# Mixing the first 128 queries by selection matmuls in a talking-heads attention kernel, and holding batch 0's score pairs to older gathers

## The chip, the cores and the metric

The kernel runs on one core of a Trainium2 chip. The metric is device time in microseconds (us) of one launch, the median over runs. TensorE is called PE, VectorE DVE, ScalarE ACT, GpSimd POOL and SyncE SP. DMA transfers are issued from the queues of SP, ACT and POOL and carried by the core's 16 DMA engines.

## The reference, cut to what matters

Attention in which the heads are mixed with each other twice (before and after the softmax), then a feed-forward layer with a squared ReLU:

```python
batch, n_heads, seq, head_dim = 8, 12, 448, 64
scores = (q @ k^T) / 8                                   # per head
scores = einsum('bhij,hg->bgij', scores, w_pre)          # heads mixed
attn = softmax(scores, axis=-1)
attn = einsum('bhij,hg->bgij', attn, w_post)             # heads mixed again
x = (attn @ v) as 3584 rows of 768
out = relu(x @ w_in)**2 @ w_out                          # 768 -> 2048 -> 768
```

## The kernel before, in words

**Score pairs.** `turn_unit` (L171) transposes q and k of two head pairs from the staged loads into PSUM (`tr_ps`); ACT copies qT and DVE copies kT to SBUF (L186). `score_pair` (L317) computes, for 128 queries and two heads, the scores of 448 keys: four matmuls (`s_ps`, L329), and two copies into the block `S` of 128 queries x 12 heads (L333, one on ACT, one on DVE). A block needs six pairs; three blocks of S are kept.

**Tiles and steps.** Mixing heads needs the heads of a query on the partition axis, whereas S has queries there. So the work goes by tiles of 10 queries (`IQ`), 45 tiles (`NT`) a batch. `gather` (L345) copies the 10 x 12 rows of a tile from S to a tile G by DMA, from SBUF to SBUF, 105 KB, on SP's queue (two of the first on ACT's). G has 8 buffers, and during the first 42 tiles (`HEAD`) six more, lent by the memory of a piece of w2 that is loaded later (`shared`, called w in the profile's rows).

A step handles two tiles. `mix` (L361) multiplies G by a block-diagonal form of w_pre (`pre`) into `m_ps` (four matmuls, L367), ACT takes the exp with its row sum (L372), DVE the reciprocal (L374), and POOL scales into `d` (L376). Two steps later (`LAG`) `unmix` (L388) multiplies by w_post and transposes (32 small matmuls, L399, `at_ps`); DVE copies into the attention tile (L404). When a part of a batch is complete, `av_unit` multiplies it by v (L199, `ot_ps`) and ACT copies to x^T (L210).

**Feed-forward.** `ffn1_unit` (L251, `h_ps`) and `ffn2_unit` (L281, `o_ps`) are cut into small units that fill TensorE in later steps, by a budget (`fill`). They use batch b's results while later batches are in attention. The weights w1 come in eight pieces, w2 in eight, over POOL's queue (`load_w1` L224, `load_w2` L236), each in a step that `at_load` names.

**Order.** PE and POOL run in the written order; DVE, ACT and SP take their instructions in program order. In each step: POOL's loads, timed units, `unmix` of two steps ago, score pairs or a turn, `mix`, gathers, `spin` (16 matmuls on the identity whose result nobody reads, in steps 0 to 9 and once before), then fillers. `scores_for` decides how many pairs a step computes, `gathers_for` issues gathers up to `gather_end`, 14 tiles ahead at first and 8 later. PSUM has eight banks, taken in turn under one tag, so a new tile waits for the reader of the tile eight allocations ago.

The lines that time the start's loads and gathers are few:

```python
HEAD = 3 * (AHEAD + 2 + MORE)                            # 42
eng = nc.scalar if k in (1, 3) else nc.sync              # gather's queue
at_load(-1 if x < 2 else 2, load_v, 0, x)                # pieces of V of batch 0
at_load(1 + x, load_w1, x)                               # w1, x = 2 to 7
if ds < PARTS[0][1] // 2 + LAG:
    spin(4)
```

Of the kernel before, what the change touches and what calls it, by code (L numbers as in the profile page):

```python
# [9 lines left out]
BF16 = mybir.dt.bfloat16  # L10
F32 = mybir.dt.float32
# [5 lines left out]
DMODEL = H * D  # L17
# [14 lines left out]
AHEAD = 6  # L32
LEAD = 14
MORE = 6
HEAD = 3 * (AHEAD + 2 + MORE)
OFF = 64 - H * (IQ // 2)
SCALE = 1.0 / 8.0
FIRST_TURN = (13, 14, 15)
# [6 lines left out]
def kernel(  # L45
# [46 lines left out]
    def wcol(w, name, eng, p0s):  # L92
# [4 lines left out]
            eng.dma_start(out=t[p0:p0 + HR, 0:H], in_=src)  # L97
        return t

    col_pre = wcol(w_pre, "col_pre", nc.sync, (OFF, 64))  # L100
    col_post = wcol(w_post, "col_post", nc.scalar, (0, 64))

# [25 lines left out]
    for t in dts:  # L128
        nc.vector.memset(t[:, S:DW], 0.0)

    shared = wts.tile([P, FT // 4 * DMODEL], BF16, name="w2_3", tag="w2_3", bufs=1)
    gts = [work.tile([P, S], BF16, name=f"G{x}") for x in range(AHEAD + 2)]
    more = [shared[:, S * x:S * x + S] for x in range(MORE)]
    for t in gts + more:
        nc.vector.memset(t[0:OFF, :], 0.0)

    def gather_tile(n):
        if n < HEAD:
            n = n % (AHEAD + 2 + MORE)
# [14 lines left out]
    w2 = [wts.tile([P, FT // 4, DMODEL], BF16, name=f"w2_{x}") for x in range(3)]  # L154

    qTs, kTs, bvecs, xts, h2ts, ats = {}, {}, {}, {}, {}, {}

# [30 lines left out]
    def av_unit(b, part, cp):  # L188
        at = ats[(b, part)]
        first = part == 0  # L190
        q0 = IQ * PARTS[b % 2][part]
        n = min(IQ * PARTS[b % 2][part + 1], S) - q0
# [43 lines left out]
    def load_w2(x):  # L236
        n = DFF // 8
        c = x % 2 * 2
        if x == 6:
            last = wts.tile([P, FT // 4 * DMODEL], BF16, name="w2_3", tag="w2_3", bufs=1)  # L240
            w2.append(last[:, :].rearrange("p (c m) -> p c m", m=DMODEL))
# [93 lines left out]
    def queries(t, y):  # L335
        return max(0, min(HQ, S - IQ * t - HQ * y))

    def span_of(s):
        b, t = s
        c = IQ * t  # L340
        return half_of(b, c) // 2, half_of(b, min(c + IQ, S) - 1) // 2

    def needs(s):
# [1 line left out]

    def gather(k):

        b, t = steps[k]
        c, end = IQ * t, min(IQ * t + IQ, S)
        g = gather_tile(k)  # L350
        eng = nc.scalar if k in (1, 3) else nc.sync
        row = OFF
        while c < end:
            n, z = divmod(half_of(b, c), 2)
            x = PR * z + c % PR
            m = min(end - c, P - x)
            eng.dma_start(out=g[row:row + H * m, :], in_=Sb[n][x:x + m, :, :])
            c, row = c + m, row + H * m
        Gs[k] = g

    def mix(k):  # L361
        pss = [bank("m_ps") for _ in range(2)]
        gs = [Gs.pop(2 * k + x) for x in range(2)]
        for y in range(2):
            for x in range(2):
                rows = slice(64 * y, 64 * y + H * queries(steps[2 * k + x][1], y) if y else 64)
                nc.tensor.matmul(pss[y][64 * x:64 * x + 64, 0:S], lhsT=pre[rows, :], rhs=gs[x][rows, :],  # L367
                                 start=True, stop=True)
        for y in range(2):
            e = work.tile([P, S], F32, name="e_sb", tag="E", bufs=3)  # L370
            sm = work.tile([P, 1], F32, name="sm", tag="sm", bufs=4)
            nc.scalar.activation(out=e[:, :], in_=pss[y][:, 0:S], func=ACT.Exp, scale=SCALE, accum_out=sm[:, 0:1])  # L372
            rc = work.tile([P, 1], F32, name="rc", tag="rc", bufs=4)
            nc.vector.reciprocal(out=rc[:, :], in_=sm[:, :])  # L374
            d = dts[(2 * k + y) % ND]
            nc.gpsimd.tensor_scalar(out=d[:, 0:S], in0=e[:, :], scalar1=rc[:, 0:1], scalar2=-1.0 / S,  # L376
                                    op0=ALU.mult, op1=ALU.add)
            dsb[(k, y)] = d

    def place_of(s):  # L380
        b, t = s
        part = sum(t >= x for x in PARTS[b % 2]) - 1
        if (b, part) not in ats:
            ats[(b, part)] = attn[(3 * b + part) % 2]
        return ats[(b, part)], 2 + IQ * (t - PARTS[b % 2][part])

    def unmix(k):

        places = [place_of(s) for s in steps[2 * k:2 * k + 2]]
        us = [bank("at_ps") for _ in range(2)]  # L390
        for y in range(2):
            d = dsb.pop((k, y))
            for r in range(VS):
                c = HR * (VS * y + r)
                for x in range(2):
                    rows = slice(64 * x, 64 * x + HR)
                    for z in range(2):
                        j = PR * (r + (R - VS) * z) if r or not z else S
                        nc.tensor.matmul(us[x][PR * z:PR * z + PR, c:c + HR], lhsT=d[rows, j:j + PR],  # L399
                                         rhs=post[rows, :], start=True, stop=True)  # L400
        for x, (at, c) in enumerate(places):
            src = us[x][:, 0:2 * VS * HR].rearrange("p (y m i) -> p m y i", y=2, i=HQ)
            dst = at[:, :, :, c:c + IQ].rearrange("p r g (y i) -> p (r g) y i", y=2)
            nc.vector.tensor_copy(out=dst, in_=src)  # L404

# [27 lines left out]
    with tc.manual_schedule(engines={PE, POOL}):  # L433
# [32 lines left out]
        issued, gathered = [NPAIR + 3], [0]  # L466
# [20 lines left out]
        def gathers_for(ds):  # L487
            while gathered[0] < min(gather_end(ds), len(steps)):
                if issued[0] < needs(steps[gathered[0]]):
                    break  # L490
                gather(gathered[0])
                gathered[0] += 1

        gathers_for(-1)
        for n in range(NPAIR, issued[0]):
            score_pair(n)
        spin(4)
        for f in loads.get(-1, []):
            f()
        for ds in range(nd + LAG):  # L500
            for i in (2 * ds, 2 * ds + 1):
                for f in loads.get(i, []):
# [19 lines left out]
            if old2:  # L522
                unmix(ds - LAG)
                for b1, t1 in old2:
                    ends = PARTS[b1 % 2]
                    if t1 + 1 in ends:
# [1 line left out]
                        for x, u in enumerate(av_units(b1, part)):  # L528
                            at_step(ds + (2 + x if b1 else 1), u)
                        if b1 == 0:  # L530
                            c = (IQ * ends[part], min(IQ * ends[part + 1], S))
# [57 lines left out]
```

The softmax here doesn't subtract the row's maximum and nothing guards it: scores larger than these inputs give would overflow.

## Time and profile before

| | |
|---|---|
| median of 13 runs | 588.24 us (583.74 to 594.48) |
| the profiled execution | 594.48 us, span 592.7 us |
| PE busy | 543.7 us (92%) |
| DVE, ACT, POOL busy | 407.4, 407.5, 399.0 us (69%, 69%, 67%) |
| DMA moved | 74.98 MB |
| chain that ended last | PE 77%, DMA 9%, ACT, DVE and POOL 3% each |
| q1 (SP's transfers) | 49.26 MB, 36.1% of 16 engines' span |
| q0 (POOL's loads) | 23.60 MB, 29.1% |
| G<-S from SP | 314 of 105.0 KB, and 15 into the lent memory |

The profile is one execution. "Busy" is the time in which an engine had an instruction at work; an idle gap is put down to what ended it (the releaser). The chain of waits goes back from the last instruction, at each step to what released it. A row of the timeline reads: start in us, length in us, engine, line of the kernel, operation, output and inputs, shape, count.

### The profile page before, as it was taken

The numbers are of one execution on the slowest core, as the hardware profiler recorded it, in microseconds if no ns is written. First come the engines' busy times: TensorE is split into PE (matmuls) and PEld (weight loads), VectorE is DVE, ScalarE is ACT, GpSimd is POOL, SyncE is SP. The second block draws the span as 40 slices with busy tenths as digits, with TensorE's granted clock in tenths as the row PEclk, the third lists the DMA queues.
The fourth block names the chain that finished last, engine by engine and source line by source line (L and its number), as shares of the span: only waits on it lengthen the run. The fifth ranks groups of instructions, "written<-read, shape, count | busy, mean of one in ns | idle before, by whom it ended". The sixth has DMA issues, their size and how long they took to land.

```text
span 592.7 us, 28172 instructions
## 1 busy us (share of the span) xinstructions
PE 543.7 (92%) x11810; PEld 310.7 (52%) x11810; DVE 407.4 (69%) x1050; ACT 407.5 (69%) x1223; POOL 399.0 (67%) x599
## 2 busy tenths in 40 slices
PE   3866698789799999999999999999999999999997
PEld 1543566554455556455555555545655555555554
DVE  5666488769777777776886777777777787765001
ACT  3656588678678866887678867896688768873420
POOL 5466559746658976788757955897678766892550
PEclk9889889889989999999999999999999999999999
DMA  9899868946974489547974599448953477442103
GB/s 138 135 219 184 179 123 146 182 82 120 202 155 93 85 163 183 115 85 123 175 157 85 98 181 184 94 86 156 182 129 78 82 145 159 82 83 56 41 11 83
DMA packets 83364, 74.98 MB, mean 127 GB/s; under 512 B 6436, under 2 KB 80164, under 8 KB 83236
## 3 DMA queue, kind: packets, MB, share of 16 engines
q1 hardware_dynamic: 51502, 49.26, 36.1%
q0 software_dynamic: 31264, 23.60, 29.1%
q8 instruction: 92, 1.51, 1.0%
q10 hardware_dynamic: 470, 0.32, 0.2%
q14 instruction: 36, 0.29, 0.1%
HBM read 47.20 MB, written 11.01 MB: 98 GB/s over the span
## 4 chain that ended last, share of the span: by engine, by line
PE 77%; DMA 9%; ACT 3%; DVE 3%; POOL 3%; issue 2%; ACTq 0%; DVEq 0%
PE o_ps L281 25%; PE h_ps L251 25%; PE at_ps L399 9%; PE ot_ps L199 6%; PE m_ps L367 6%; DMA G<-S 6%; PE s_ps L329 4%; PE tr_ps L182 2%; DMA w<-S 2%; DMA qkst<-in_q_dram 1%; POOL d L376 1%; DVE at L404 1%; ACT e_sb L372 1%; ACT xt L210 1%; POOL w L232 1%
## 5 line engine op out<-in xcount | busy, mean ns | idle before, releaser
L376 POOL TENSOR_SCALAR d<-e_sb,rc 128x448 bf16<-128x448 f32 x360 | 226.3, 639 | 154.2 <-DVE rc L374 153.0
L404 DVE CAST at<-at_ps 128x480 bf16<-128x480 f32 x360 | 219.8, 650 | 69.7 <-PE at_ps L399 63.3
L372 ACT ACTIVATE e_sb<-m_ps 128x448 f32<-128x448 f32 x360 | 195.6, 559 | 22.1 <-PE m_ps L367 16.7
L251 PE MATMUL h_ps<-xt,w 128*128 128x448 bf16 (+2 forms) x960 | 165.1, 321 | 1.9 <-DVE at L404 0.8
L281 PE MATMUL o_ps<-w,h 128*128 128x384 bf16 (+1 forms) x1024 | 163.2, 329 | 0.0
L260 POOL TENSOR_TENSOR h<-hr 128x448 bf16<-128x448 f32 (+2 forms) x136 | 113.7, 845 | 15.7 <-ACT hr L258 15.7
L251 PEld LDWEIGHTS <-w 128*128 128x128 bf16 x960 | 81.3, 100 | 79.2 <-issue 30.3
L281 PEld LDWEIGHTS <-h 128*128 128x128 bf16 (+1 forms) x1024 | 82.6, 101 | 71.5 <-issue 26.5
L333 ACT CAST S<-s_ps 128x448 bf16<-128x448 f32 (+1 forms) x174 | 90.8, 542 | 41.9 <-PE s_ps L329 39.5
L333 DVE CAST S<-s_ps 128x448 bf16<-128x448 f32 (+1 forms) x174 | 104.3, 613 | 0.9 <-PE s_ps L329 0.9
L399 PEld LDWEIGHTS <-d 60*64 60x64 bf16 x5760 | 64.6, 110 | 58.6 <-issue 36.6
L399 PE MATMUL at_ps<-post,d 60*64 60x60 bf16 x5760 | 85.3, 195 | 10.0 <-issue 5.6
L258 ACT ACTIVATE hr<-h_ps 128x448 f32<-128x448 f32 (+2 forms) x160 | 74.5, 487 | 20.0 <-PE h_ps L251 14.2
L374 DVE RECIPROCAL rc<-sm 128x1 f32<-128x1 f32 x360 | 52.6, 157 | 46.5 <-ACT e_sb L372 44.1
L367 PE MATMUL m_ps<-G,pre 64*64 64x448 bf16 (+2 forms) x684 | 74.1, 362 | 9.4 <-DMA G<-S 5.9
L372 ACT ACTIVATION_READ_ACCUMULATOR e_sb<-m_ps 128x1 f32 x360 | 78.7, 219 | 0.0
L210 ACT ACTIVATE xt<-ot_ps,bvec 128x160 bf16<-128x160 f32 (+3 forms) x144 | 44.7, 385 | 44.8 <-PE ot_ps L199 35.7
L329 PE MATMUL s_ps<-kT,qT 64*64 64x448 bf16 x672 | 65.5, 377 | 0.7 <-issue 0.3
L288 DVE COPY osb<-o_ps 128x384 f32<-128x384 f32 x48 | 26.0, 547 | 36.8 <-PE o_ps L281 36.6
L199 PE MATMUL ot_ps<-at,v 128*64 128x160 bf16 (+4 forms) x1152 | 45.9, 229 | 0.1
L199 PEld LDWEIGHTS <-v 128*64 128x64 bf16 x1152 | 38.4, 109 | 13.7 <-issue 12.4
L367 PEld LDWEIGHTS <-pre 64*64 64x64 bf16 x720 | 28.2, 107 | 30.2 <-issue 22.7
(42 smaller groups left out, 214.1 us busy)
## 6 DMA issues: line engine op xcount, KB each, us to landing
G<-S SPq DMA_DIRECT2D x314, 105.0 KB
out_dram<-osb SPq DMA_DIRECT2D x48, 192.0 KB
v<-in_v_dram POOLq DMA_DIRECT2D x32, 192.0 KB, 5.6
qkst<-in_k_dram POOLq DMA_DIRECT2D x24, 224.0 KB, 5.9
qkst<-in_q_dram POOLq DMA_DIRECT2D x24, 224.0 KB, 6.4
w<-in_moe_w_in_dram POOLq DMA_DIRECT2D x8, 384.0 KB, 11.3
w<-in_moe_w_out_dram POOLq DMA_DIRECT2D x8, 384.0 KB, 8.0
w<-S SPq DMA_DIRECT2D x15, 105.0 KB
```

The lines of the kernel that those rows point to most:

```text
L199: nc.tensor.matmul(ps[64 * hh:64 * hh + 64, TW * y + c0:TW * y + 2 + n], lhsT=vs[b][:, g, r, :], rhs=at[:, r, g, c0:2 + n], start=(y == 0 ...
L251: nc.tensor.matmul(ps[:, 0:n], lhsT=w1[ft // 4][:, c2, ft % 4 * 128:ft % 4 * 128 + 128], rhs=xts[b][:, c2, c0:c1], start=(c2 == 0), stop=( ...
L258: nc.scalar.activation(out=hr[:, 0:n], in_=ps[:, 0:n], func=ACT.Relu)
L260: square.tensor_tensor(out=h2ts[(b, ft)][:, c0:c1], in0=hr[:, 0:n], in1=hr[:, 0:n], op=ALU.mult)
L281: nc.tensor.matmul(dst, lhsT=h2ts[(b, ft)][:, mt * 128:mt * 128 + ROWS[mt]], rhs=w2[ft // 4][:, ft % 4, n2 * 384:(n2 + 1) * 384], start=(f ...
L329: nc.tensor.matmul(pss[hh][PR * z:PR * z + PR, 0:S], lhsT=qTs[b][rs, p, PR * j:PR * j + PR], rhs=kTs[b][rs, p, :], start=True, stop=True)
L333: copy(out=Sb[n][z0:z1, 2 * p + hh, :], in_=pss[hh][z0:z1, 0:S])
L367: nc.tensor.matmul(pss[y][64 * x:64 * x + 64, 0:S], lhsT=pre[rows, :], rhs=gs[x][rows, :], start=True, stop=True)
L372: nc.scalar.activation(out=e[:, :], in_=pss[y][:, 0:S], func=ACT.Exp, scale=SCALE, accum_out=sm[:, 0:1])
L376: nc.gpsimd.tensor_scalar(out=d[:, 0:S], in0=e[:, :], scalar1=rc[:, 0:1], scalar2=-1.0 / S, op0=ALU.mult, op1=ALU.add)
L399: nc.tensor.matmul(us[x][PR * z:PR * z + PR, c:c + HR], lhsT=d[rows, j:j + PR], rhs=post[rows, :], start=True, stop=True)
L404: nc.vector.tensor_copy(out=dst, in_=src)
```

## The change

The first 13 tiles of batch 0 (`FIRST`) cover queries 0 to 127 in another arrangement: tile t holds queries 5t to 5t+4 and the same ones of the second 64. They are no longer gathered. Instead `mix` takes S itself as the moving operand: for each of the 12 heads and each half of 64 queries, a matmul whose weights `z` choose five queries and spread each to the 12 mixed heads with the factor w_pre[h, g]. A tile takes 24 matmuls that accumulate in `m_ps`; a step with two such tiles takes 48 where there were four. Tiles from 13 on are gathered as before, 10 queries each from query 128.

The weights z are built on the chip: the w_pre row is loaded to all partitions (a new small DMA on SP, ahead of col_pre's), DVE adds the two halves of the identity (`idz`), and products of the two fill z: four of 128 x 1536 elements on DVE, ahead of the first kT copy, and one of 128 x 3072 on POOL, after the first two pieces of w1 and ahead of V. They lie in memory of w2 pieces, which are loaded later.

Also moved: V of batch 0 (pieces 2, 3) and w1 pieces 2, 3 go ahead of step 0; w1 pieces 4 to 7 to steps 0 to 3; the six memsets of the lent memory from DVE's start to POOL in steps 0 to 2; the spins of steps 0 to 5 and the one before them are dropped (steps 6 to 9 keep theirs). Since PE tiles hold queries of two halves, their `at` copies are two of 240 elements instead of one of 480. The score pairs of batch 0 count as free only those blocks whose gathers had been issued three steps (tile pairs) earlier (`SETTLE`), and none before step 7. All gathers go over SP. The first part of batch 0 ends at query 158 instead of 160.

```diff
-HEAD = 3 * (AHEAD + 2 + MORE)
+FIRST = 13
+SETTLE = 3
+FQ = 128
+ROUND = AHEAD + 2 + MORE
+HEAD = FIRST + 2 * ROUND
+ZH = 4
+ZW = 64 * H
...
+    shared = wts.tile([P, FT // 4 * DMODEL], BF16, name="w2_3", tag="w2_3", bufs=1)
+    wpre = shared[:, MORE * S:MORE * S + 2 * H * H].bitcast(F32)
+    nc.sync.dma_start(out=wpre,
+                      in_=bass.AP(tensor=w_pre.tensor, offset=w_pre[0, 0:1].offset, ap=[[0, P], [1, H * H]]))
...
-    for t in gts + more:
+
+    for t in gts:
         nc.vector.memset(t[0:OFF, :], 0.0)
...
-        return min(2 * ds + AHEAD + 2 + MORE, max(HEAD + AHEAD + 2, 2 * ds + AHEAD + 2))
+        return min(max(2 * ds, FIRST - 2) + ROUND, max(HEAD + AHEAD + 2, 2 * ds + AHEAD + 2))
+
+    def query(b, t):
+        if b == 0 and t < FIRST:
+            return min(HQ * t, FQ // 2 - HQ)
+        return min(FQ + IQ * (t - FIRST) if b == 0 else IQ * t, S)
+
+    def by_pe(k):
+        return k < FIRST
...
+    zs = [wts.tile([P, ZH * ZW], BF16, name=f"w2_{x}", tag=f"w2_{x}", bufs=1) for x in range(3)]
+    idz = shared[:, MORE * S + 2 * H * H:MORE * S + 2 * H * H + 64]
+    nc.vector.tensor_tensor(out=idz, in0=ident[:, 0:64], in1=ident[:, 64:P], op=ALU.add)
+
+    def z_unit(x, eng, h0=0, h1=ZH):
+        eng.tensor_tensor(out=zs[x][:, ZW * h0:ZW * h1].rearrange("p (h q g) -> p h q g", h=h1 - h0, g=H),
+                          in0=idz.unsqueeze(1).unsqueeze(3).to_broadcast([P, h1 - h0, 64, H]),
+                          in1=wpre.rearrange("p (h g) -> p h g", g=H)[:, ZH * x + h0:ZH * x + h1, :].unsqueeze(2).to_broadcast([P, h1 - h0, 64, H]),
+                          op=ALU.mult)
+
+    for x in range(2):
+        for h in range(0, ZH, 2):
+            z_unit(x, nc.vector, h, h + 2)
...
     def gather(k):
 
+        if by_pe(k):
+            return
...
-        eng = nc.scalar if k in (1, 3) else nc.sync
+        eng = nc.sync
...
     def mix(k):
         pss = [bank("m_ps") for _ in range(2)]
-        gs = [Gs.pop(2 * k + x) for x in range(2)]
+        pair = (2 * k, 2 * k + 1)
+        gs = [None if by_pe(n) else Gs.pop(n) for n in pair]
+        for h in range(H):
+            for y in range(2):
+                rows = slice(64 * y, 64 * y + 64)
+                for x, n in enumerate(pair):
+                    if by_pe(n):
+                        c = ZW * (h % ZH) + H * query(0, n)
+                        m = min(64, ZH * ZW - c)
+                        nc.tensor.matmul(pss[y][64 * x:64 * x + m, 0:S], lhsT=zs[h // ZH][rows, c:c + m],
+                                         rhs=Sb[0][rows, h, :], start=(h == 0), stop=(h == H - 1),
+                                         skip_group_check=True)
...
+            if by_pe(2 * k + x):
+                for y in range(2):
+                    j = c + FQ // 2 * y
+                    nc.vector.tensor_copy(out=at[:, :, :, j:j + HQ].rearrange("p r g i -> p (r g) i"), in_=src[:, :, y, :])
+                continue
...
-            at_load(-1 if x < 2 else 2, load_v, 0, x)
+            at_load(-2, load_v, 0, x)
...
-            at_load(1 + x, load_w1, x)
+            at_load(-2 if x < 4 else 2 * x - 8, load_w1, x)
...
+        for f in loads.get(-1, []):
+            f()
+        z_unit(2, nc.gpsimd)
+        for f in loads.get(-2, []):
+            f()
+        for x, t in enumerate(more):
+            at_load(x, nc.gpsimd.memset, t[0:OFF, :], 0.0)
...
-            full = sum(gathered[0] >= x for x in lasts)
+            seen = past[-SETTLE] if ds <= NT // 2 and len(past) >= SETTLE else gathered[0]
+            full = sum(seen >= x for x in lasts) if 2 * ds >= FIRST else 0
...
-        spin(4)
-        for f in loads.get(-1, []):
-            f()
...
-            if ds < PARTS[0][1] // 2 + LAG:
+            if FIRST // 2 <= ds < PARTS[0][1] // 2 + LAG:
                 spin(4)
```

More of the change, by code (lines that the diff above doesn't have):

```diff
@@ L129 @@
         nc.vector.memset(t[:, S:DW], 0.0)
-    shared = wts.tile([P, FT // 4 * DMODEL], BF16, name="w2_3", tag="w2_3", bufs=1)
     gts = [work.tile([P, S], BF16, name=f"G{x}") for x in range(AHEAD + 2)]
     more = [shared[:, S * x:S * x + S] for x in range(MORE)]
-    for t in gts + more:
+    for t in gts:
         nc.vector.memset(t[0:OFF, :], 0.0)
@@ L138, in gather_tile @@
         if n < HEAD:
-            n = n % (AHEAD + 2 + MORE)
+            n = (n - FIRST) % ROUND
             return more[n - AHEAD - 2] if n >= AHEAD + 2 else gts[n]
@@ L143, in gather_end, with bounds @@
     def gather_end(ds):
-        return min(2 * ds + AHEAD + 2 + MORE, max(HEAD + AHEAD + 2, 2 * ds + AHEAD + 2))
+        return min(max(2 * ds, FIRST - 2) + ROUND, max(HEAD + AHEAD + 2, 2 * ds + AHEAD + 2))
[5 more added lines that the diff above has]
+        return k < FIRST
+    def bounds(b, part):
+        ends = PARTS[b % 2][part:part + 2]
+        return tuple(query(b, t) if t else 0 for t in ends)
     attn = [atp.tile([P, VS, H, TW], BF16, name=f"at{x}") for x in range(2)]
@@ L153 @@
     w1 = [wts.tile([P, NPAIR, DFF // 4], BF16, name=f"w1_{x}") for x in range(4)]
-    w2 = [wts.tile([P, FT // 4, DMODEL], BF16, name=f"w2_{x}") for x in range(3)]
+    w2 = []
+    zs = [wts.tile([P, ZH * ZW], BF16, name=f"w2_{x}", tag=f"w2_{x}", bufs=1) for x in range(3)]
[9 more added lines that the diff above has]
+            z_unit(x, nc.vector, h, h + 2)
     qTs, kTs, bvecs, xts, h2ts, ats = {}, {}, {}, {}, {}, {}
@@ L190, in av_unit @@
         first = part == 0
-        q0 = IQ * PARTS[b % 2][part]
-        n = min(IQ * PARTS[b % 2][part + 1], S) - q0
+        q0, q1 = bounds(b, part)
+        n = q1 - q0
         c0 = 0 if first else 2
@@ L238, in load_w2 @@
         c = x % 2 * 2
-        if x == 6:
-            last = wts.tile([P, FT // 4 * DMODEL], BF16, name="w2_3", tag="w2_3", bufs=1)
-            w2.append(last[:, :].rearrange("p (c m) -> p c m", m=DMODEL))
+        if x % 2 == 0:
+            t = wts.tile([P, FT // 4 * DMODEL], BF16, name=f"w2_{x // 2}", tag=f"w2_{x // 2}", bufs=1)
+            w2.append(t[:, :].rearrange("p (c m) -> p c m", m=DMODEL))
         nc.gpsimd.dma_start(out=w2[x // 2][:, c:c + 2, :],
@@ L333, in score_pair, with queries @@
             copy(out=Sb[n][z0:z1, 2 * p + hh, :], in_=pss[hh][z0:z1, 0:S])
-    def queries(t, y):
-        return max(0, min(HQ, S - IQ * t - HQ * y))
+    def queries(s, y):
+        return max(0, min(HQ, S - query(*s) - HQ * y))
     def span_of(s):
         b, t = s
-        c = IQ * t
+        if b == 0 and t < FIRST:
+            return 0, 0
+        c = query(b, t)
         return half_of(b, c) // 2, half_of(b, min(c + IQ, S) - 1) // 2
@@ L346, in gather @@
     def gather(k):
+        if by_pe(k):
+            return
         b, t = steps[k]
-        c, end = IQ * t, min(IQ * t + IQ, S)
+        c = query(b, t)
+        end = min(c + IQ, S)
         g = gather_tile(k)
-        eng = nc.scalar if k in (1, 3) else nc.sync
+        eng = nc.sync
         row = OFF
@@ L362, in mix @@
         pss = [bank("m_ps") for _ in range(2)]
-        gs = [Gs.pop(2 * k + x) for x in range(2)]
+        pair = (2 * k, 2 * k + 1)
[10 more added lines that the diff above has]
+                                         skip_group_check=True)
         for y in range(2):
             for x in range(2):
-                rows = slice(64 * y, 64 * y + H * queries(steps[2 * k + x][1], y) if y else 64)
+                if gs[x] is None:
+                    continue
+                rows = slice(64 * y, 64 * y + H * queries(steps[2 * k + x], y) if y else 64)
                 nc.tensor.matmul(pss[y][64 * x:64 * x + 64, 0:S], lhsT=pre[rows, :], rhs=gs[x][rows, :],
@@ L384, in place_of @@
             ats[(b, part)] = attn[(3 * b + part) % 2]
-        return ats[(b, part)], 2 + IQ * (t - PARTS[b % 2][part])
+        return ats[(b, part)], 2 + query(b, t) - bounds(b, part)[0]
     def unmix(k):
@@ L402, in unmix @@
             src = us[x][:, 0:2 * VS * HR].rearrange("p (y m i) -> p m y i", y=2, i=HQ)
+            if by_pe(2 * k + x):
+                for y in range(2):
+                    j = c + FQ // 2 * y
+                    nc.vector.tensor_copy(out=at[:, :, :, j:j + HQ].rearrange("p r g i -> p (r g) i"), in_=src[:, :, y, :])
+                continue
             dst = at[:, :, :, c:c + IQ].rearrange("p r g (y i) -> p (r g) y i", y=2)
@@ L464 @@
                     at_load(NT * b + 46 + 2 * x, load_v, b + 1, x)
+        for f in loads.get(-1, []):
[5 more added lines that the diff above has]
+            at_load(x, nc.gpsimd.memset, t[0:OFF, :], 0.0)
         nd = len(steps) // 2
-        issued, gathered = [NPAIR + 3], [0]
+        issued, gathered, past = [NPAIR + 3], [0], []
         spans = [span_of(s) for s in steps]
@@ L492, in gathers_for @@
                 gathered[0] += 1
+            past.append(gathered[0])
         gathers_for(-1)
@@ L530 @@
                         if b1 == 0:
-                            c = (IQ * ends[part], min(IQ * ends[part + 1], S))
+                            c = bounds(0, part)
                             at_step(ds + 1, (0, lambda c=c: filler.extend(ffn1_units(0, *c))))
```

## The prediction

> **What bounds the kernel now.** I read the page's 40 slices first: where is TensorE not full?
>
> ```profile
> PE   3866698789799999999999999999999999999997
> PEclk9889889889989999999999999999999999999999
> DMA  9899868946974489547974599448953477442103
> ```
>
> TensorE sits at 9 from slice 12 on (about 180 us) and falls short only before, in slices 0 to 5 (0 to 89 us) most of all. The DMA engines are at 9 there. The table by stretches (first number: length; then the busy time of PE, PEld, DVE, ACT, POOL, the granted clock, the DMA share, GB/s) sizes it:
>
> ```profile
> 0.00:20.00 20.00, 9.00 (x228) 5.30 (x228) 13.03 (x48) 8.36 (x15) 7.91 (x17) 1.00 0.94 139
> 20.00:40.00 20.00, 13.17 (x323) 8.65 (x327) 11.90 (x32) 10.86 (x33) 14.64 (x22) 0.91 0.98 175
> 40.00:60.00 20.00, 13.96 (x353) 9.00 (x346) 13.01 (x34) 12.71 (x41) 12.35 (x20) 0.92 1.04 194
> 60.00:80.00 20.00, 14.84 (x458) 11.40 (x457) 12.48 (x31) 12.90 (x41) 9.94 (x17) 0.83 0.74 157
> 200.00:300.00 100.00, 98.83 (x2201) 54.51 (x2201) 75.44 (x192) 74.94 (x227) 75.13 (x112) 1.00 0.75 140
> ```
>
> TensorE loses 29 us of the first 80 and 1 us of a later 100. So a microsecond won or lost in the first 80 reaches the end one for one. What releases the stage is in the chain of waits (start, length, what):
>
> ```profile
> 33.47 12.60 DMA G<-S
> 46.07 0.04 issue
> 46.11 0.38 PE m_ps L367 x3
> ...
> 47.74 11.57 DMA w<-S
> ```
>
> Gathers that take about 12 us from issue to landing, since they share full DMA engines with the weight loads. In TensorE's timeline the last mix matmul of step 6 begins at 39.4 and that of step 12 at 59.36 us: 3.3 us a step over steps 7 to 12, against 2.2 us from step 2 (25.60) to step 3 (27.79), where no gather was late.
>
> **The change part by part.**
>
> Gathers removed: 13 of the first 25, at 105 KB. The hardware queue q1 moved 49.26 MB in 36.1% of 592.7 us, 4.3 us per MB, so 13 gathers are 1.4 MB or 6 us of all 16 engines. The loads move earlier too: the second half of V and the next w1 pieces were issued at 24 us and later, behind step 0's d, and now come before it. I take steps 7 to 12 as no longer gather-bound, since tiles 13 to 24 go out in one go at step 1, some five steps ahead of their first use. Next late there: DVE, with two at copies (0.61 each, back to back), two reciprocals (0.16) and one or two S copies (0.57), 2.1 to 2.7 us. I take 2.35 a step, and 3.2 for step 10, whose two ot_ps units (1.87 us) sit in it: 6 steps = 15.0 us instead of 20. Gain 5 us. Bounds: 0 (the gathers that remain wait as before) and 6.6 (2.2 a step).
>
> Mixes added: steps 0 to 5 get 48 matmuls each, step 6 gets 24. The near row is the spin group, the same 64x64 quarters with 448 columns: 16 in 0.78 us (21.51 until the next group at 22.29), or 2.3 us for 48. Six and a half mixes are 15 us of TensorE; 112 spin matmuls (5.5 us) and 26 gather matmuls (1 us) go. It is on the path: nothing else is left to wait for. Step 0 is 2.3. Steps 1 to 3 add 32 at_ps (0.41), two score pairs (0.4), and a wait of 0.3, because the mix reuses the banks that the last exps free 1.05 us after the last mix: 3.45 each. Step 4 is 3.25, step 5 2.75, step 6 1.9. Sum 20.5 us from the first mix to the end of step 6's, against 19.4 (20.33 to 39.7) now. Bounds: 19 without the bank wait, 24 if the quarters did not overlap as the spins do.
>
> The at copies of the PE tiles are split in two: four per step for two. A 480-element copy is 0.65 us, a small one from PSUM (64x6) 0.15, so a half is 0.4 and DVE has 1.6 + 0.3 + 1.15 = 3.05 us in steps 1 to 3, under TensorE's 3.45. It costs nothing while the mixes hide it; uncovered it would be 0.3 us a step.
>
> Building z: this decides. DVE gets four products of 128x1536 ahead of the first kT copy in its order, POOL one of 128x3072 ahead of V's loads and w1's next pieces. DVE's rows: 0.32 us for 160 elements, 0.27 for 128 where undisturbed; at about 1 ns an element 1536 is 1.7 us, four are 6.8. POOL: 934 ns for 448 and 455 for 160, 1.66 ns an element, so 3072 is 5.3 us (bounds: 5, and 10.6 if runs of 12 elements halve its rate). Both wait for post's DVE product, which ends at 8.02 us, for idz (0.2), and for the small w_pre load, which no row shows (I take it as landed by 8; its neighbour col_post landed at 7.8). Queued behind them on DVE: kT's first copy, at 8.75 us now, without which no score matmul starts.
>
> ```profile
> 7.80 0.22 DVE L118 TENSOR_TENSOR post<-stripe_post,col_post 128x60 bf16<-128x60 f32 x1 [1.53 <-DMA col_post<-in_w_post_dram]
> 8.75 0.62 DVE L186 COPY kT<-tr_ps 128x896 bf16<-128x896 bf16 x1 [0.72 <-PE tr_ps L182]
> ```
>
> Do the two engines build z side by side? The trace says no:
>
> ```profile
> 89.16 1.31 POOL L376 TENSOR_SCALAR d<-e_sb,rc 128x448 bf16<-128x448 f32 x2 [0.29 <-DVE rc L374]
> 89.23 0.73 DVE L260 TENSOR_TENSOR h<-hr 128x160 bf16<-128x160 f32 x1
> ...
> 93.81 0.30 DVE L260 TENSOR_TENSOR h<-hr 128x160 bf16<-128x160 f32 x1
> ```
>
> The same DVE product takes 0.73 us under a POOL operation and 0.30 alone: it stands still until POOL's first d is done and then goes ahead of the second. The Trainium skill (SBUF — State Buffer, Who interferes with whom) says this of a VectorE instruction with two SBUF inputs against a GpSimd instruction that reads SBUF: the second to issue blocks until the first has finished. The rule speaks against this change. With both engines at full rate the four DVE products end at 8.2 + 6.8 = 15.0; under the lock, with POOL's product let in after DVE's first, as DVE was let in between the two d's, at 15.0 + 5.3 = 20.3, and 0.5 more for POOL's DMA issues (a product at 107.25 took 0.63 beside one). I take 20.8. The trace does not show DVE's own products queued back to back, so that POOL waits for all four stays possible.
>
> From there DVE has three kT copies (0.62), two S copies (1.15) and six more (3.80 for seven) until the bank of the first mix is free: 6.3 us. First mix at 27.1 instead of 20.3. Half-speed TensorE after its idle stretch: the spin group at 16.61 took 1.49 us before the next group, twice the later 0.78, so I add 1.0 to the first mixes (bounds 0 and 2.3).
>
> Sum: 27.1 + 20.5 + 1.0 = 48.6 at the end of step 6 (now 39.7, so 8.9 later), + 15.0 = 63.6 at step 12 (now 59.7: 3.9 later). Between 60 and 80 us the granted clock is 0.83 after idle gaps; with steadier TensorE work I give back 1.0 of the 2.5 us (14.84 x 0.17) that this can cost. Net 3 us lost. The profiled execution lasted 594.48 us (span 592.7 and 1.8 around it), the slowest of 13 runs; it would become 597.5. On the median of 588.24 the same 3 us give **591.2**.
>
> SETTLE, the changed ends of the attention parts (158 for 160 columns) and the moved memsets (0.25 us each, from DVE's idle start to POOL) I cost at nothing: the score pairs stand on TensorE one step later at most, from step 13 on, and LEAD leaves them ahead of need. Uncovered, one late pair is 0.4 us of TensorE and 0.6 of an S copy; bounds 0.5 us either way.
>
> **The rivals.**
>
> Products side by side, or POOL last: kT's first copy at 15.0, first mix at 21.3, step 6 ends at 42.8, step 12 at 57.8 (1.9 earlier), and the clock gives 1.0: 585.3. For it: DVE starts first and its products need no further wait. Against: the rows at 89 us.
>
> Relief of the DMA engines reaches further: TensorE stood still 1.77 and 3.17 us in at_ps at 66 and 71 us with nothing in the profile to wait for, while loads and gathers filled the engines. If lighter traffic takes these 4.9 us away as well, the forecast becomes 586.3 and the first rival 580.4. Against: the traffic between 60 and 80 us is nearly the same in both kernels.
>
> POOL's product is twice as slow on runs of 12 elements: + 5.3, 596.5. It decides as soon as the first kT copy comes later than about 18 us (the 3 us by which 20.8 may shrink before the loss is gone); for it, that no row shows such a form.
>
> The change doesn't do what it says: the gathers that are left still land late and steps 7 to 12 keep 3 us or more. Then only the later start remains, + 6 to + 9 at step 12, 594 to 597. Against it: six steps of lead, and 6 us less traffic.
>
> **How the numbers follow.** About 0.5% (2.9 us) is what a measurement of this kernel can tell from no change. Chances: forecast 0.37, forecast with the stalls gone 0.10, side by side 0.22, side by side with the stalls gone 0.14, slow POOL 0.09, gathers still late 0.08. Over 2.9 us faster: all of the 0.14, near half of the 0.22 (at 585.3 the bound itself), and 0.12 from the tails of the others: 0.36. Over 2.9 us slower: half of the 0.37, the 0.17 of the two slow ones: 0.37 with a rounding up. Within: 0.27. The range goes from the fastest case to just over the slow POOL: 580.5 to 597.5; the likeliest case alone spans 588 to 595.
>
> **What would show it.** The four z products on DVE should span some 12 us with one of them at 7 us rather than 1.7, and the first kT copy should start at about 20.8 (forecast) or 15 (rival). The first mix: 27 or 21. TensorE should be busy from then to the end of step 6, each mix near 2.3 us; no m_ps matmul should wait for a gather in steps 7 to 12, and the steps should take near 2.35. The forecast is wrong if kT is early, if the mixes take over 3 us, or if 60 to 80 us keeps its TensorE share of 74% or rises far above it.

## The result, and the profile after

The changed kernel takes 599.83 us (median of 11 runs, 595.24 to 603.02), the kernel before 587.5 (48 runs). The ratio is 1.0212, with a 95% interval of 1.0182 to 1.0241: slower by 12.5 us, against a forecast of 3 and a range that ended at 597.5. Ratios are made from undisturbed runs alone and medians from all runs, so the two need not agree; in e12 below, whose ratio counts 12 of 22 runs, they do not.

The profiled execution after has a span of 599.9 us and lasted 601.93 us. Its slices first, in the order of those shown of before:

```profile
PE   1398789789999999999999999999999999999997
PEclk9997969899999999999999999999999999999999
DMA  8978857985995389646964499548953477442103
```

TensorE has 1 in the first slice where it had 3, and 3 in the second where it had 8; the DMA engines are no longer at 9 throughout the start. The stretches, with the columns of the table of before:

```profile
0.00:20.00 20.00, 1.93 (x112) 1.70 (x113) 12.57 (x31) 3.10 (x3) 15.01 (x19) 1.00 0.75 114
20.00:40.00 20.00, 15.43 (x346) 9.98 (x349) 15.88 (x34) 11.47 (x30) 10.69 (x19) 1.00 0.88 123
40.00:60.00 20.00, 17.14 (x430) 11.58 (x424) 12.87 (x43) 9.10 (x30) 11.02 (x18) 0.84 0.89 172
60.00:80.00 20.00, 15.07 (x495) 11.36 (x492) 14.53 (x37) 13.29 (x43) 13.40 (x23) 0.84 0.87 161
200.00:300.00 100.00, 98.83 (x2156) 53.50 (x2155) 76.23 (x194) 76.25 (x229) 76.24 (x113) 1.00 0.72 136
```

TensorE is busy for 1.93 us of the first 20, where it had 9.00, and does more than before in each of the next three; from 200 us on both kernels are full. What held it up stands in DVE's and POOL's timelines (two views, so two fences):

```profile
10.57 0.22 DVE L124 TENSOR_TENSOR pre<-stripe_pre,col_pre 128x60 bf16<-128x60 f32 x1 [6.08 <-DMA col_pre<-in_w_pre_dram]
11.14 0.22 DVE L128 TENSOR_TENSOR post<-stripe_post,col_post 128x60 bf16<-128x60 f32 x1 [0.35 <-DMA col_post<-in_w_post_dram]
11.50 11.94 DVE L183 TENSOR_TENSOR w<-w 128x1536 bf16<-128x1536 bf16 x4
23.37 1.14 DVE L222 COPY kT<-tr_ps 128x896 bf16<-128x896 bf16 x2
```

```profile
11.55 6.94 POOL L183 TENSOR_TENSOR w<-w 128x3072 bf16<-128x3072 bf16 x1 [3.85 <-DVE w L180]
```

Read them from the brackets. DVE stood idle 6.08 us for col_pre's small load, which had landed before 6.05 in the kernel before; so post's product ran at 11.14 instead of 7.80 and the z products began at 11.50. These took 11.94 us for four, while POOL's product ran beside them. The first two kT copies came at 23.37, not 8.75 and 11.60.

From there the mixes went as planned, in TensorE's timeline:

```profile
29.35 2.91 PE L413 MATMUL m_ps<-S,w 64*64 64x448 bf16 x48
...
44.84 2.48 PE L413 MATMUL m_ps<-S,w 64*64 64x448 bf16 x48
...
54.83 1.71 PE L488 MATMUL spin_ps<-ident 64*64 64x448 bf16 x16 [2.86 <-ACT S L369]
```

The first mix is at 29.35; step 6's last mix matmul begins at 49.73 (not shown). The last row is in step 7: the spins there waited 2.86 us for their PSUM bank, which ACT's S copy had not read yet. Why that copy was late is in the list of waits (engine, line, what it waited for: us, times, longest):

```profile
ACT S L369 <- DMA G<-S: 2.9, 1, 2.9
PE spin_ps L488 <- ACT S L369: 2.9, 1, 2.9
```

A copy of a new S block that waits for gathers: no such row with a gather as releaser was in before. No mix of steps 7 to 12 waits for a gather any more.

Where the two kernels stand in time, by the start of POOL's first d of a step (us, from the traces; "before, second" is a second profile of the same kernel, taken with the experiments):

| step | 0 | 6 | 12 | 18 | 40 | 179 |
|---|---|---|---|---|---|---|
| before, as shown | 22.8 | 41.1 | 59.2 | 83.9 | 146.4 | 540.0 |
| before, second | 23.4 | 40.1 | 58.1 | 79.2 | 139.3 | 534.7 |
| after | 33.1 | 51.2 | 70.3 | 93.2 | 154.2 | 547.2 |

The loss is there at step 0 (10 us), is 11 to 12 at step 12, and against the second profile it stays: 14.9 at step 40, 12.5 at step 179. By the end of step 12's last mix matmul, which the forecast counted, the change stands at 67.5 against 59.7 and 58.6: 7.8 and 9.0 us late. That is less, because in the kernel before the second tile of step 12 came late, behind the first d.

### The profile page after: what moved, and what is told of

Read it like the earlier page. It is cut to its first block, busy times and chain, and to the rows that moved or that the text cites. A ratio compares the mean times of both kernels' runs of the same rounds, so it can differ in the third digit from the quotient of the medians.

```text
span 599.9 us, 28505 instructions
## 1 busy us (share of the span) xinstructions
PE 548.4 (91%) x11984; PEld 315.7 (53%) x11984; DVE 421.8 (70%) x1062; ACT 407.3 (68%) x1223; POOL 408.4 (68%) x606
## 4 chain that ended last, share of the span: by engine, by line
PE 77%; DVE 7%; DMA 6%; ACT 4%; issue 3%; POOL 1%; SPq 1%; ACTq 0%; DVEq 0%
PE o_ps L317 24%; PE h_ps L287 24%; PE at_ps L453 9%; PE ot_ps L235 7%; PE m_ps L421 5%; PE s_ps L365 4%; DMA G<-S 4%; DVE at L463 2%; DVE w L183 2%; PE tr_ps L218 2%; ACT xt L246 2%; ACT e_sb L426 2%; DMA col_post<-in_w_post_dram 1%; DMA w<-S 1%; DVE h L296 1%
## 5 line engine op out<-in xcount | busy, mean ns | idle before, releaser
L463 DVE CAST at<-at_ps 128x480 bf16<-128x480 f32 x347 | 211.9, 650 | 64.1 <-PE at_ps L453 53.8
L287 PE MATMUL h_ps<-xt,w 128*128 128x448 bf16 (+3 forms) x960 | 165.5, 320 | 6.5 <-ACT hr L294 2.5
L287 PEld LDWEIGHTS <-w 128*128 128x128 bf16 x960 | 81.2, 99 | 83.0 <-issue 33.8
L296 POOL TENSOR_TENSOR h<-hr 128x448 bf16<-128x448 f32 (+3 forms) x136 | 113.6, 844 | 15.7 <-ACT hr L294 15.7
L294 ACT ACTIVATE hr<-h_ps 128x448 f32<-128x448 f32 (+3 forms) x160 | 74.4, 486 | 22.2 <-PE h_ps L287 13.2
L421 PE MATMUL m_ps<-G,pre 60*64 60x448 bf16 (+2 forms) x670 | 73.3, 359 | 4.9 <-ACT xt L246 2.2
L246 ACT ACTIVATE xt<-ot_ps,bvec 128x160 bf16<-128x160 f32 (+5 forms) x144 | 44.7, 385 | 45.8 <-PE ot_ps L235 36.3
L365 PE MATMUL s_ps<-kT,qT 64*64 64x448 bf16 x672 | 64.0, 372 | 10.7 <-DVE kT L222 9.8
L235 PE MATMUL ot_ps<-at,v 128*64 128x160 bf16 (+5 forms) x1152 | 45.9, 229 | 0.1
L218 PE MATMUL tr_ps<-ident,qkst 64*64 64x64 bf16 x1344 | 19.6, 203 | 17.9 <-DMA qkst<-in_q_dram 12.3
```

The lines of the kernel that those rows point to most:

```text
L287: nc.tensor.matmul(ps[:, 0:n], lhsT=w1[ft // 4][:, c2, ft % 4 * 128:ft % 4 * 128 + 128], rhs=xts[b][:, c2, c0:c1], start=(c2 == 0), stop=( ...
L294: nc.scalar.activation(out=hr[:, 0:n], in_=ps[:, 0:n], func=ACT.Relu)
L296: square.tensor_tensor(out=h2ts[(b, ft)][:, c0:c1], in0=hr[:, 0:n], in1=hr[:, 0:n], op=ALU.mult)
L365: nc.tensor.matmul(pss[hh][PR * z:PR * z + PR, 0:S], lhsT=qTs[b][rs, p, PR * j:PR * j + PR], rhs=kTs[b][rs, p, :], start=True, stop=True)
```

## The experiments

Theory: what is queued on DVE ahead of the score copies (the wait for the loads, the z products, POOL's product that stops them) delays the first mix, and this delay reaches the end. Rivals: the 48 mix matmuls a step cost more than the gathers they replace; or the S copies that wait for gathers end the stage.

**POOL's product away** (e1):

```diff
-        z_unit(2, nc.gpsimd)
+        nc.gpsimd.memset(zs[2][:, :], 0.0)
```

> The changed kernel with POOL's z product (128x3072) replaced by a memset to zero, so the mixes of the first 128 queries leave out heads 8 to 11; every other instruction stays. Theory (the z products ahead of the first kT copy[...] delay the first mix): the four DVE products take about 7 us instead of 11.94, the first kT copy comes at 18.4 instead of 23.37, and the time falls by 4 to 5 us, to about 595. Rival (the PE-bound mixes of steps 0 to 6 are the cost, the start is not): 599 to 600. Rival (the wait of the S copies for gathers is what ends the stage): 597 to 600, with the copy in step 7 waiting longer by what the start gained.

Measured: 594.47 us, ratio 1.0113 (1.0042 to 1.0184). DVE's timeline of this kernel:

```profile
12.55 6.76 DVE L183 TENSOR_TENSOR w<-w 128x1536 bf16<-128x1536 bf16 x4
19.23 1.15 DVE L222 COPY kT<-tr_ps 128x896 bf16<-128x896 bf16 x2
```

The same four products: 6.76 us instead of 11.94. POOL's product alone cost DVE 5.2 us, and about 5.8 us (0.0099 of 587; the intervals just meet) of the time went with it. POOL's loads of V went out earlier as well (from 10.91 instead of 18.44), but step 0's d was already 4.1 us earlier and step 12's 4.7, so most of the gain is there at the first mix. That the start doesn't count is refuted.

**All products away** (e2): memsets for DVE's four too.

> The changed kernel with all five z products replaced by memsets, so the first 128 queries are not mixed at all (zeros), while every mix matmul is still issued. Theory (start): first kT copy at 9 to 12 us (still behind the small w_pre loads), first mix at 16 to 18 instead of 29.35, time 12 us lower, near 588, equal to the kernel before or a little under it. Rival (PE-bound mixes): 597 to 600. Rival (S copies wait for gathers): the gain is cut to about 6 us, 594, because gathers start with S block 1 and their landing does not move as far.

Measured: 590.33 us, ratio 1.0050 (1.0025 to 1.0075): 9.5 us of the 12.5 are the products. The first kT copy came at 11.78, step 0's d at 24.7 instead of 33.1, step 12's at 60.0 instead of 70.3.

```profile
11.78 0.62 DVE L221 COPY kT<-tr_ps 128x896 bf16<-128x896 bf16 x1
```

**The w_pre load away** (e3):

```diff
-    nc.sync.dma_start(out=wpre, in_=...)
+    nc.vector.memset(wpre, 0.1)
```

> The changed kernel with the w_pre load to 128 partitions left out (its place in memory is set to 0.1 by a memset), so the first 128 queries are mixed with constant weights. Theory (the new load of 128 small rows holds up the small col loads and the q and k loads): col_pre and col_post land by 8 us again instead of 11, the z products start at 8.3 instead of 11.5, time 3 us lower, 596.5. Rival (col loads are late by chance or by another transfer): z starts at 11.5 and the time stays at 599 to 600.

Measured: 596.44 us, ratio 1.0138 (1.0081 to 1.0195): 4.3 us less than the change, though the intervals overlap. The time is as expected, the start is not: in DVE's timeline the wait for col_pre shrinks from 6.08 to 2.87 us, but the products begin at 9.71, not at 8.3:

```profile
7.51 0.22 DVE L123 TENSOR_TENSOR pre<-stripe_pre,col_pre 128x60 bf16<-128x60 f32 x1 [2.87 <-DMA col_pre<-in_w_pre_dram]
9.71 11.94 DVE L182 TENSOR_TENSOR w<-w 128x1536 bf16<-128x1536 bf16 x4
```

That is 1.8 us earlier than in the change, and so is the first mix (27.55). The rest of the 4.3 us shows only behind that (step 12's d is 2.4 us earlier, step 18's 4.7), and these traces do not tie it to the load.

**Neither load nor products** (e5): both edits together.

> The changed kernel with neither the w_pre load nor the z products (memsets in their place), so the first 128 queries come out as zeros; all mix matmuls stay. Theory (the start alone costs): first kT copy at 9, first mix at 17 to 18, time 3 us under the version with memsets and load (590.3), so 587, equal to the kernel before. Rival (mixes on TensorE cost more than the gathers they replace): it stays at 589 to 590, above the kernel before, though nothing holds up its start.

Measured: 587.78 us, ratio 1.0009 (0.9978 to 1.0041). TensorE's first mix came before that of the kernel before (20.33):

```profile
18.80 3.14 PE L411 MATMUL m_ps<-S,w 64*64 64x448 bf16 x48
```

The building of z, load and products, is 11.9 us, all of the loss to within the interval's 2 us. What remains of the change is worth nothing in sum, though it holds a gain:

**The early loads** by themselves (e4, and again with more rounds as e14), put into the kernel before:

```diff
-            at_load(-1 if x < 2 else 2, load_v, 0, x)
+            at_load(-1, load_v, 0, x)
-            at_load(1 + x, load_w1, x)
+            at_load(-1 if x < 4 else 2 * x - 8, load_w1, x)
```

> The kernel before with one part of the change alone: V of batch 0 and w1 pieces 2 and 3 loaded before step 0, the other w1 pieces in steps 0, 2, 4 and 6 halved to steps 0 to 3; the gathers stay. If the gap of the DMA engines from 17 to 25 us was lost capacity, gathers of steps 7 to 12 land earlier: 584 to 586. If the early loads only get in front of the first gathers: first mix 3 to 6 us later, 590 to 593. My guess is the latter, 590.

> The kernel before with the early loads alone, once more, with more rounds: 582 to 584, 0.6 to 1% under the kernel before, if the first result (582.43 against 587.38) holds; 585 or more would make it a chance.

Measured: 582.43 us, ratio 0.9894 (0.9816 to 0.9972), and 586.17 us, ratio 0.9950 (0.9922 to 0.9977). The second rests on more runs: some 3 us faster than the kernel before by the ratio, which is clear of 1, and 2 us by the medians (586.17 against 588.2). Its median lies above the 585 from which the expectation would call the first result a chance, so of the first 5 us about half is left. My guess of 590 was wrong. The first mix did come later, but in TensorE's timeline that was the one long wait:

```profile
24.40 0.59 PE L367 MATMUL m_ps<-G,pre 64*64 64x448 bf16 x4 [5.07 <-DMA G<-S]
```

Afterwards gathers were late by 0.7 us at most and step 12's d came at 56.4.

**Early loads taken out of the change** (e7), the same edit the other way:

> The changed kernel with V of batch 0 and w1 loaded at the steps of the kernel before (V pieces 2 and 3 in step 1, w1 from step 1 on); everything else as changed. If the early loads are a gain that the rest of the change hides (alone they gave 5 us), the time rises to 602 to 605. If the start of the changed kernel leaves the DMA engines idle long enough for either order, it stays at 600.

Measured: 605.16 us, ratio 1.0307 (1.0254 to 1.0361), 5.6 us slower than the change as it is. In its trace the z products began 1.6 us later (13.14), and the S copy of step 7 waited longer for gathers, 6.2 us for 2.9; so part of the 5.6 is this wait:

```profile
ACT S L369 <- DMA w<-S: 6.2, 1, 6.2
```

**V early, w1 from step 0 on** (e12), in the kernel before:

```diff
+            at_load(-1, load_v, 0, x)
+            at_load(0 if x < 4 else x - 3, load_w1, x)
```

> The kernel before with all of V of batch 0 loaded before step 0, w1 pieces 2 and 3 in step 0, and 4 to 7 in steps 1 to 4. The early loads of V and w1 together gave 5 us though they held up the first mix by 3 us (24.4 for 21.5). If the gain comes from the DMA engines' gap before 25 us and the 3 us can be kept as well, the time is 580 to 582. If w1 has to be in that gap for the gain, 584 to 587.

Measured: 586.57 us, ratio 0.9945 (0.9919 to 0.9970), like e14's; but the medians, 586.57 and 586.97, are only 0.4 us apart, so a gain of e12 is not shown. The 3 us of the first mix were not kept either: step 0's d was at 25.6. The edit does less than was meant. `at_load` counts tiles, two a step, so w1 pieces 2 to 4 fall in step 0, and POOL issued them ahead of that step's d:

```profile
13.34 1.52 POOL L232 DMA_DIRECT2D w<-in_moe_w_in_dram  x2 [0.47 <-DMA qkst<-in_q_dram]
15.27 0.77 POOL L232 DMA_DIRECT2D w<-in_moe_w_in_dram  x1 [0.41 <-DMA w<-in_moe_w_in_dram]
25.62 1.25 POOL L376 TENSOR_SCALAR d<-e_sb,rc 128x448 bf16<-128x448 f32 x2 [9.58 <-DVE rc L374]
```

So e12 is nearly e4 again, and which of the early loads, V or w1, delays the first gathers stays open.

**Fewer mix matmuls** (e6): on top of e5, heads 0 to 3 only.

```diff
-        for h in range(H):
+        for h in range(ZH):
```

> As the version with neither load nor z products, and besides only heads 0 to 3 are mixed for the first 128 queries: 16 matmuls a step for 48. If the mixes set the pace of steps 0 to 6 (2.3 us each, two thirds of it gone: 1.5 us a step, 10 us in all), the time falls to 579 to 582, below the early loads alone (582.4). If the exps, copies and POOL set it anyway, it falls by 2 to 4 us only.

Measured: 593.81 us, ratio 1.0105 (1.0063 to 1.0147): slower than e5 with three times the matmuls, which neither case had foreseen. Steps 0 to 6 did go faster, d of step 6 at 34.2 instead of 42.8, and then nothing moved until 45.9. The waits between 15 and 70 us:

```profile
ACT S L367 <- DMA G<-S: 10.0, 1, 10.0
PE spin_ps L486 <- ACT S L367: 10.0, 1, 10.0
DVE S L367 <- DMA G<-S: 8.6, 1, 8.6
```

This is the wait of step 7 again, now 10 us. The first copy into the fourth S block waits in this program for all eight semaphores that the gathers signal. The block whose memory it takes, that of the first 128 queries, is read by no gather any more; so what it waits for must be gathers of other tiles, issued since step 1. Faster mixes only run into it sooner.

**The fourth block's pairs held until step 10** (e8), in the changed kernel; and with e6's mixes (e9) and e5's (e13):

```diff
-            full = sum(seen >= x for x in lasts) if 2 * ds >= FIRST else 0
+            full = sum(seen >= x for x in lasts) if 2 * ds >= FIRST + 7 else 0
```

> The changed kernel with the score pairs of the fourth block held until step 10 instead of 7. The S copy in step 7 waited 2.9 us for a gather, though no gather reads the block that it overwrites. If that wait is only for the gathers just issued (the last ones when the block is given back), it moves to step 10 and stays, 599 to 600. If it is for gathers that have landed by step 10, 2 to 3 us are gained: 597.

> As the version with neither load nor z products and 16 matmuls a step for 48 (heads 4 to 11 of the first 128 queries left out), and the score pairs of the fourth block held until step 10. That version's S copies stood 10 us in step 7 for gathers. Theory: taking the mixes away did not pay because the gathers of tiles 13 to 25, all issued from step 1 on, then are what step 7 waits for; without the copies in their way the steps go on until the first gathered tile is needed, so the wait falls to some 3 to 6 us and the time to 585 to 589. Rival (the shorter mixes hurt through TensorE's clock, half speed from 39 to 49 us): no gain, 592 to 594.

> As the version with neither load nor z products (first 128 queries come out as zeros; all 48 mix matmuls a step), and the score pairs of the fourth block held until step 10. If the mixes on TensorE take the early loads' 5 us back: 586 to 588, as without the hold. If the wait of the S copies for gathers does: 582 to 584. I expect mostly the mixes, since step 6 ended at 42.8 against 40.3 with gathers and early loads, and the wait was short there: 585.5.

Measured: e8 597.5 us, ratio 1.0156 (1.0105 to 1.0207), no S copy waiting for a gather in its list; e9 582.03, ratio 0.9892 (0.9843 to 0.9942); e13 587.52, ratio 0.9971 (0.9945 to 0.9997). So the hold is worth 12.5 us where the mixes are short. In the change as it is the ratios differ by 3.3 us and where the start is free by 2.2, but both times the intervals overlap, and in e5's trace no S copy waits for a gather, so the 2.2 is not tied to that wait. In e9 3.9 us of the wait remained, at step 10; the rival of the half-speed clock is refuted, since e9 has the same short mixes and gained. For e13 against e14 (0.9971 and 0.9950) the intervals overlap: with a free start and no wait, 48 matmuls a step cost about what the gathers cost, within some 3 us. The two traces show how: from the first mix to the end of step 6's, e13 took 23.2 us and e14 15.5, but e13, with no gather to wait for, began 6.0 us earlier (18.4 for 24.4); at the end of step 12 it was 2.1 us behind.

**Products behind the first score copies** (e11), the whole computation:

```diff
+        for x in range(2):            # after the transposes and first score pairs
+            for h in range(0, ZH, 2):
+                z_unit(x, nc.vector, h, h + 2)
```

> The changed kernel (whole computation) with the four DVE products written after the first transposes and score pairs. In the built order one product stays ahead of the first kT copy, two come between the first and the second, one ahead of the third. If what counts is all that is queued ahead of the block's last copies, the first mix comes at 28 instead of 29.35 and the time falls by 1 to 2 us, to 598. If the first kT copy is what counts, it falls by 8 us, to 592.

Measured: 599.43 us, ratio 1.0195 (1.0148 to 1.0242), no gain to be told from none. Its DVE timeline says why, and prices the products one by one:

```profile
13.75 1.76 DVE L183 TENSOR_TENSOR w<-w 128x1536 bf16<-128x1536 bf16 x1
15.42 0.62 DVE L219 COPY kT<-tr_ps 128x896 bf16<-128x896 bf16 x1
15.96 8.06 DVE L183 TENSOR_TENSOR w<-w 128x1536 bf16<-128x1536 bf16 x2
23.94 0.61 DVE L219 COPY kT<-tr_ps 128x896 bf16<-128x896 bf16 x1
...
25.54 1.74 DVE L183 TENSOR_TENSOR w<-w 128x1536 bf16<-128x1536 bf16 x1
27.20 0.61 DVE L219 COPY kT<-tr_ps 128x896 bf16<-128x896 bf16 x1
```

A product alone takes 1.76 us; two beside POOL's take 8.06. The first kT copy came 8 us earlier than in the change, the third 1.4 us later, and the time followed the third. The products began 2.25 us later in this execution; counted from there, the third copy gained 0.9 us and the first mix 0.8, so the new order can be worth little at most. (This also corrects a sentence above: DVE's order is not simply the written one. Within the dependences the build places DVE's instructions itself; it put these four between the copies.)

**The kernel before, again** (e10):

> The kernel before, unchanged, for a second trace of it. The profiled execution shown before lasted 594.48 us against a median of 587. Theory: the 7 us lie in the first 120 us (late gathers, TensorE standing with nothing to wait for); in a typical run step 12's d starts near 56 instead of 59.2 and step 40's near 141 instead of 146.4, and from step 40 on nothing differs.

Measured: 589.1 us, span 587.3. The difference from the shown profile lies where expected, in the early steps, step 40 at 139.3 instead of 146.4, but little of it is in late gathers: step 12's d came at 58.1, not near 56, and steps 12 to 18 took 21.1 us for 24.7. TensorE's 1.77 and 3.17 us with nothing to wait for, which fall in those steps, have no counterpart here.

The three-step lag of `SETTLE` was not run: with `gathered[0]` in its place the built program has the same order on every engine as the change, so in this kernel that half of the change does nothing. Only its other half, no such pairs before step 7, can act.

## Why the prediction was wrong

By its own steps:

- **Building z** was right in its mechanism and nearly in its size. Forecast: four products at 1.7, stopped by POOL's for 5.3, and 0.5 for POOL's DMA issues, 12.6 us in all. Measured: 11.94 (6.76 without POOL's). The 0.5 did not come: the last two products took 1.75 us each beside POOL's DMA issues. The Trainium skill's rule (SBUF — State Buffer, Who interferes with whom) held here: POOL's row of 6.94 us is one DVE product's wait, 1.7, and its own 5.2, so POOL was let in after the first. The rival of products side by side is refuted by e1, that of a slow POOL product by the same 5.2.
- **When the products start** failed: "I take it as landed by 8", and the products at 8.2. They began at 11.50, 3.3 us late. I had counted the added DMA as one that must land, not as one that the others wait for. By e3, 1.8 of the 3.3 us go with the change's own w_pre load, first on SP's queue. The other 1.5 no run explains: without the load col_post was still waited for until 9.35, and 8.62 in the second profile of before.
- **From kT to the first mix**: forecast 6.3, measured 6.0 (23.37 to 29.35). **Mixes**: forecast 20.5 + 1.0, measured 20.7 (29.35 to 50.1, the end of step 6). Right, without the 1.0 for a half-speed start: the granted clock was 1.00 up to 40 us. Step 6 ended 1.5 us later than forecast.
- **Steps 7 to 12** took 17.4 us (to 67.5), not 15.0: "SETTLE ... I cost at nothing", with bounds of 0.5 us, failed. The forecast did not ask what the first copies into the fourth block wait for once they may be issued; 2.9 us of S copies waited for the gathers just issued. What is left, the steps without that wait, fits 15 (14.3 in e8). But the gain was put down to the removed gathers, and the early loads alone bring all of it without touching a gather: 14.8 us in e4 and 13.9 in e14, by the same measure, against 20.0 in before.
- **"I give back 1.0"** came in part against the execution that the sum was made on (7.8 us late at step 12, the spans 7.2 apart), but not by the clock: from 60 to 80 us it was granted at 0.84, where it had been 0.83, and no trace here shows that steadier work raises it. Against the second profile nothing came back: from step 12 to step 40 the change took 83.9 us and that profile 81.2.
- **The base** is the largest part. The sum was made against an execution of 594.48 us, the slowest of all 48, and the difference carried over to the median. The two profiled executions lie 7.4 us apart, the kernels 12.5. Between steps 12 and 40 the shown profile took 87.2 us and the second, of 589.1 us, 81.2: the change doesn't mend what was lost there, so its difference to most runs is the larger one. With one second profile, what most runs lose there stays an inference.

Errors of the sum up to step 12: 3.9 us (start of the products 3.3, products -0.7, kT to first mix -0.3, mixes -0.8, steps 7 to 12 2.4). Of the other 5.6 of 9.5, about 5 are the base and the rest the give-back.

Two of the forecast's own signs spoke against it: the products started late, and from 60 to 80 us TensorE kept its share (15.07 us, 75%, for 74%). Of the rivals, lighter traffic did not take TensorE's idle 4.9 us away: 2.64 and 1.96 us were left. "Gathers still late" came nearest: its + 6 to + 9 at step 12 holds the 7.8, but what waited for a gather was an S copy, not a mix. A slow POOL product did not occur. The direction of the loss was seen, at 0.37 against 0.36 for a gain; its size was not.

What stays open: the price of the mixes themselves against the gathers lies within some 3 us; the traces of e13 and e14 put it at about 2 us of loss, the times leave its sign open. And no version here builds z without cost, so that the idea as a whole can pay has not been shown: with a free start and the hold it equals, within the intervals, the early loads alone, which need none of it. Of whole computations only the early loads in the kernel before came out faster, by 0.5% in e14's ratio.

## What to carry to other kernels

A setup step costs what it delays, so list everything queued behind it on its engine up to the last instruction that the first real work needs; moving it behind the first of several such copies gained next to nothing (e11). An added DMA at the start can also hold up the loads around it (e3). When a change bundles several edits, cost each alone: the gain of the early loads had been put down to the removed gathers (e4, e14). A profile is one execution: before carrying a difference from it to a median, ask whether it lost time that typical runs don't lose.

## What was not expected of the hardware

- A small load on one queue delayed the small loads on another: col_post, on ACT's queue, was waited for until 11.14 us or later in all six kernels with the w_pre load on SP's queue (11.14 to 13.39), and until 9.35 at most in the five changed kernels without it (9.14 to 9.35). In the five traces without the rest of the change it was 7.80 to 8.62.
- DVE's product stands still under a POOL instruction, but not under two in a row: POOL's next one queues behind DVE (0.73 us for 0.30 under two d's, in the rows at 89 us ahead). One of 1.76 us became, with a second, 8.06 beside POOL's 5.2.
- TensorE stands for 1 to 4 us, waiting for nothing that the profile shows, mostly where some hundred small matmuls (transposes, at_ps) follow each other while the DMA engines are busy: 1.77 and 3.17 us in before, 2.64 and 1.96 in after, 3.98 in e4. The packets of the DMA queues show what these waits have in common. All 45 of over 1 us, in all 16 traces, end 1.2 to 1.6 us after a packet has come in on queue q8, although one comes only every 6 us or so. The page of before lists this queue as follows (packets, MB, share):

```profile
q8 instruction: 92, 1.51, 1.0%
```

That is 16 KB a packet, and one packet for some 257 of TensorE's 23,620 matmuls and weight loads. TensorE waiting for its own next instructions would fit all this, but no run here varied it.
